# A planner's order searched anew with at most eight transfers in flight: attention and an MLP mixer on one core

## The chip, the cores and the metric

The kernel runs on one core of one Trainium2 chip. The metric is the device time of one execution in microseconds (us). Before the change three runs took 642.58, 644.96 and 646.78 us, so the median is 644.96 us.

## The reference, cut to what matters

Attention over 4 batches, 8 heads, 576 positions and head width 64, with a bias that a tiny network makes of the distance between positions; then a mixer over positions and an MLP over channels:

```python
scores = 0.125 * q @ k.T                          # per batch and head
x = log1p(abs(i - j)) / log1p(max(i, 1))          # 576 x 576
bias = relu(x[..., None] @ w1 + b1) @ w2          # 32 hidden, 8 heads; the same for all batches
attn = softmax(scores + bias)                     # sum + 1e-9 below the line
x = concat_heads(attn @ v)                        # 4 x 576 x 512, float32
h = relu(x.T @ w_tok1) @ w_tok2                   # mixes positions, 256 wide
u = x + h.T
out = u + relu(u @ w_ch1) @ w_ch2                 # 1536 wide; the weights are float64
```

## The kernel before, in words

All work goes through one planner. The program first lists steps (`add`), each with the engines that could run it and an estimated cost, a due time, the steps it comes after, and the buffers and PSUM banks that it takes and frees. `Plan.order` then plays the steps through on paper: at each turn it takes, on the engine that could start soonest, the step with the smallest due time among those that could start within `SLACK` of the first. The instructions are emitted in the order that comes out, so each engine's queue, SP's queue of transfers included, is fixed when the program is built. Nothing reorders at run time. Due times are the numbers of the table `DUE`, found by a search on the plan.

The stages, and the names that the text below uses:

- **Bias stage.** 36 blocks. For each, three rectifications on DVE (L494) and one on ACT (L492), 16 matmul instructions in the profile (L511), an eviction on ACT (L517) and a store of the block to DRAM (`bd<-slots`, L522). Meanwhile the k and q of the first units are loaded (L741, issued from ACT's queue) and split into a high part on ACT (L369: `kh`, `qh`) and a low part on DVE or POOL (L384: `kl`, `ql`).
- **Attention.** 16 units; a unit is one pair of heads of one batch. It loads k, q and v (`kk`, `qq`, `tv`, L741 and L745, from ACT's queue) and, for the first unit of a pair of heads, six pieces of the bias (`slots<-bd`, L716 and L719, from SP's queue). For each of five blocks of 128 rows: scores (L783), bias and row minimum on DVE (L792), exponential on ACT (L805), turning by transposing matmuls (L834, evicted by ACT at L837 and DVE at L840) or by a DMA transpose (L823), and the product with v (L861 to L863). Then the mixer over positions (L911 to L922), and the unit's result is stored (`um<-x`, L940, and `ul<-x`, L942, from SP's queue).
- **Weights.** Beside attention the float64 weights come in as words (L365, `keep<-wt`, `keep<-wc`) and are put together as float32 (L630, L632, L635, L638), their largest value taken (L359), and split.
- **Channels.** Five blocks of tokens. The stored rows are loaded, scaled and split (L1075, L1078), turned by DMA transposes (L1086), multiplied by the first weight (L1102 to L1104), and by the second (L1193 to L1195, or L1287 to L1289 with the reads at L1298 and L1301). Results leave at L1177.

Two things of the planner matter here. The first is how it treats a transfer: it assumes one wire on which transfers follow each other, and an issue costs its queue 0.4 us, or 0.35 us on ACT. The second is `keep_warm` (L318): where the plan has PE wait more than 1 us, it puts small matmuls of 128x256 on a free bank to fill that time.

In the built program every transfer, from either queue, signals one of eight semaphores in turn, and its issuing instruction first waits until the transfer that used that semaphore before has landed: about the one eight issues back, counted over both queues. This wait is in the program before and after the change; the planner before did not know of it.

Of the kernel before, what the change touches and what calls it, by code (L numbers as in the profile page):

```python
# [36 lines left out]
SLACK = 0.099  # L37
STAY = 136.61
# [17 lines left out]
      'dlo2': {'P': (1.9, 114.7), 'V': (0.67, -522.92)},  # L56
      'late': {'P': (0.7, 2520.57), 'A': (0.58, 2227.24)},
      'klow': {'P': (1.5, -153.69), 'V': (0.83, -54.59)},
      'zlow': {'P': (1.25, -1770.91), 'V': (0.6, 1857.34)},
      'twhole': {'P': (2.4, -3419.57), 'V': (1.21, -578.92)},  # L60
      'tsum': {'P': (3.0, 1762.24), 'V': (1.72, 444.73)},
      'tlow': {'P': (2.1, 1907.96), 'V': (1.15, 1327.33)},
      'oall': {'P': (2.7, 789.47), 'V': (1.2, 4220.75)},
      'norm': {'V': (0.35, -2033.47), 'A': (0.88, -1163.02)},
      'over': {'A': 0.65, 'V': (0.72, 409.34)},
      'vh': {'P': (0.7, 1664.84), 'V': (0.4, 1349.27), 'A': (0.6, 81.13)},
      'vl': {'P': (1.36, 488.82)}}
DUE = {'tie': 2658.62,
       'blk': -1001.52,
       'blkn': 37.41,  # L70
       'rect': -384.79,
       'bmm': -1271.54,
       'over': -2767.83,
       'put': -1632.04,
       'bl': 332.43,
       'bln': 47.87,
       'sums': 1060.11,
       'sumsn': 150.59,
       'measw': 219.61,
       'measwn': 13.46,  # L80
       'amax': 160.39,
       'scales': 261.94,
       'scalet': -1140.4,
       'scalec': -1768.42,
       'fill': -1334.98,
       'fill1': 1025.41,
       'tok': -998.98,
       'tokn': 86.58,
       'dec1': -291.1,
       'dec2': -123.37,  # L90
       'dec3': 843.13,
       'dec4': 377.41,
       'dec5': -1426.64,
       'load_k': 561.15,
       'load_q': -669.99,
       'split_k': -741.14,
       'first_k': -1091.54,
       'first_q': -317.21,
       'split_q': -105.53,
       'load_v': -1139.54,  # L100
       'prep_v': 2207.84,
       'prep_vh': -916.66,
       'prep_vl': -2285.41,
       'scores': -464.7,
       'biased': -310.8,
       'exp': -159.63,
       'hi': -1117.91,
       'lo': -515.95,
       'turn': -229.06,
       'flip': -1722.06,  # L110
       'fliphi': -1800.75,
       'flip2': -669.83,
       'fliplo': -46.83,
       'back': 1260.45,
       'norm': -696.83,
       'mix0': -1911.87,
       'mix1': 971.0,
       'relu': -3172.82,
       'mix2': -1913.89,
       'mix2b': -42.35,  # L120
       'store': -2510.07,
       'w1': 99.4,
       'w1n': 24.56,
       'U0': 902.85,
       'U0n': -448.96,
       'U1n': -76.52,
       'U1': 387.42,
       'U2': -1098.39,
       'Un': -26.37,
       'U3': 650.82,  # L130
       'U4': 532.91,
       'u1': 2642.21,
       'u2': -968.46,
       'u3': -735.61,
       'u4': -2938.78,
       'u5': 426.22,
       'G': 158.67,
       'G0': 1626.57,
       'G0n': -111.49,
       'g1': -1574.27,  # L140
       'g2': -177.12,
       'ur': -828.11,
       'H': 2543.86,
       'e1': 668.96,
       'e2': -24.44,
       'e3': -1194.05,
       'e4': 996.36,
       't2': 1217.88,
       't3': -1551.03,
       't4': -1836.99,  # L150
       'T1': -1314.84,
       'Tn': -167.36,
       'rd': 141.44,
       'urs': 643.45,
       'un': 116.14,
       'v1': -1357.25,
       'v2': 412.08,
       'v3': -88.48,
       'v4': -155.45,
       'v5': -1146.62,  # L160
       'v6': 564.59,
       'v7': -216.22,
       'v8': -2074.96,
       'w2m': -255.93,
       'w2mn': 54.04}
# [27 lines left out]
class Plan:  # L193
# [17 lines left out]
    def order(self):  # L211
        room = {k: [(0.0, i) for i in range(n)] for k, n in self.rooms.items()}
        at = dict(FIRST)
        wire, port, port_by = 4.0, 0.0, None
# [11 lines left out]
        while len(out) < len(self.steps):  # L226
            best = None
            for e, steps in ready.items():
                first, can = None, []
                for s in steps:  # L230
                    t = max(at[e], s.ready, *(h.busy[0] + (0.0 if h.busy[1] == e else 0.15) for h in s.bank))
                    if e == "P" or e == "V" and s.port:
                        t = max(t, port)
                    held = 0.0
# [33 lines left out]
            if s.wire:  # L268
                wire = max(wire, t + 0.56) + s.wire
                s.end = wire + (1.53 if s.gate else 1.93)  # L270
                at[e] = t + (ISSUE if e == "A" else 1.25 if s.gate else 0.4)
            else:
                if e == "P" and port_by is not None and port_by.engine == "V" and t <= port:
                    s.behind = port_by
                at[e] = s.end = t + cost
                if e == "P" or e == "V" and s.port:
                    port, port_by = s.end, s
# [18 lines left out]
def attention_mixer(ctx, tc, qT, kT, v, cst, lg, ident, wt1, wt2, wc1, wc2, out, dump=None):  # L296
# [111 lines left out]
    with tc.manual_schedule():  # L408
# [301 lines left out]
        def bias_load(hp, t0):  # L710
# [3 lines left out]
            for c in range(NCH):  # L714
                bias_in[hp, c] = [add(wire("bias", 2.0), t0 + DUE["bln"] * c,
# [14 lines left out]
        def unit(u):  # L730
# [37 lines left out]
            for c in range(NCH + 1):  # L768
# [17 lines left out]
                lead = chain("scores", add({"T": 0.9 if c < NCH else 0.95}, t + DUE["scores"], scores, after=[*ready, *bias_in[hp, c], drawn],  # L786
# [24 lines left out]
                if dma:  # L811
# [13 lines left out]
                    s = add({"A": 0.45}, t + DUE["hi"], rest_hi, after=exps[:1], take=[p2], use=[z])  # L825
# [571 lines left out]
```

## Time and profile before

| | us |
|---|---|
| median of 3 runs | 644.96 |
| lowest, highest | 642.58, 646.78 |
| profiled execution | 641.31 |
| its span on the core | 639.4 |
| PE busy | 617.8 (97%) |
| DVE busy | 501.8 (78%) |
| ACT busy | 410.0 (64%) |
| POOL busy | 266.4 (42%) |

The span reaches from the first instruction to the last; the remaining 1.9 us of the profiled execution lie around it. PE is TensorE's matmuls, DVE VectorE, ACT ScalarE, POOL GpSimd, SP the engine that only issues transfers; ACTq and SPq are the queues of ACT and SP. Idle time of an engine costs only where the end depends on it.

### The profile page before, as it was taken

How to read it: one execution, taken by the hardware profiler on the slowest of the kernel's cores; microseconds unless marked ns; L12 is line 12 of the kernel's file. 1: busy time of each engine (PE TensorE's matmuls, PEld its weight loads, DVE VectorE, ACT ScalarE, POOL GpSimd, SP SyncE). 2: the span in 40 equal slices, each digit the busy share in tenths (PEclk: the TensorE clock that was granted, in tenths of full speed). 3: DMA queues.
4: the chain of work that ended last, by engine and by line, in shares of the span. 5: the costliest groups of instructions: out<-in, count | busy, mean ns of one | idle time of the engine just before them, and what ended most of it. 6: DMA issues, size and time to landing. Idle time of an engine off the chain costs nothing.

```text
span 639.4 us, 18066 instructions
## 1 busy us (share of the span) xinstructions
PE 617.8 (97%) x7226; PEld 457.3 (72%) x7226; DVE 501.8 (78%) x1242; ACT 410.0 (64%) x751; POOL 266.4 (42%) x299
## 2 busy tenths in 40 slices
PE   9999888998999999999999999999999999999997
PEld 4445777896999998989899874444444468646886
DVE  7998899987899999999999867994775894266222
ACT  7998888876798999989888525542542641244110
POOL 1004777953575888778653700001233422022211
PEclk9999999998999999999999999999999999999999
DMA  8999665798676965466544795664221115400221
GB/s 314 403 365 336 132 143 146 264 332 191 192 160 194 287 125 138 112 144 185 132 95 86 240 290 213 180 176 116 52 64 40 63 34 132 99 1 0 81 86 33
DMA packets 88515, 101.92 MB, mean 159 GB/s; under 512 B 49392, under 2 KB 58864, under 8 KB 88432
## 3 DMA queue, kind: packets, MB, share of 16 engines
q1 hardware_dynamic: 78784, 80.04, 44.6%
q10 hardware_dynamic: 9648, 20.75, 11.1%
q8 instruction: 56, 0.92, 0.6%
q14 instruction: 27, 0.22, 0.1%
HBM read 69.69 MB, written 20.05 MB: 140 GB/s over the span
## 4 chain that ended last, share of the span: by engine, by line
PE 72%; DVE 9%; ACT 7%; DMA 5%; POOL 4%; issue 3%; ACTq 0%; SPq 0%; POOLq 0%; DVEq 0%
PE pair L783 7%; PE bank L834 6%; PE bank L1103 5%; PE bank L1104 5%; PE bank L1102 5%; PE bank L1289 4%; PE bank L1287 4%; PE bank L1288 4%; PE pair L511 4%; DVE z L792 3%; DVE t2a L840 2%; PE pair L1104 2%; PE bank L1195 2%; PE bank L1194 2%; PE pair L1103 2%
## 5 line engine op out<-in xcount | busy, mean ns | idle before, releaser
L805 ACT ACTIVATE z<-z,mx 128x576 f32<-128x576 f32 (+1 forms) x120 | 92.7, 780 | 12.1 <-DVE mx L792 7.6
L792 DVE CUSTOM_DVE_ANT_0 z<-pair,slots 128x576 f32<-128x576 f32 (+1 forms) x120 | 89.3, 756 | 4.2 <-PE pair L783 3.6
L840 DVE SCALAR_TENSOR_TENSOR t2a<-bank,t2a 128x384 f16<-128x384 f32 (+1 forms) x150 | 79.6, 538 | 6.6 <-ACT t2a L837 5.1
L834 PE MATMUL bank<-id,z 128*128 128x128 f32 x469 | 76.0, 283 | 6.2 <-DVE t2a L840 2.7
L837 ACT ACTIVATE t2a<-bank 128x384 f16<-128x384 f32 (+1 forms) x150 | 70.2, 473 | 16.8 <-PE bank L834 11.2
L783 PE MATMUL pair<-kh,qh 64*128 64x288 f32 (+1 forms) x288 | 62.5, 347 | 4.7 <-DVE mx L792 4.0
L834 PEld LDWEIGHTS bank<-id,z 128*128 128x128 f32 x469 | 50.0, 141 | 15.8 <-issue 4.8
L1103 PE MATMUL bank<-slots 128*128 128x512 f16 (+1 forms) x168 | 58.6, 349 | 1.3 <-DMA slots<-wd 1.3
L861 PE MATMUL bank<-vh,t2a 128*128 128x65 f16 x558 | 58.6, 194 | 0.0
L1102 PE MATMUL bank<-slots 128*128 128x512 f16 (+1 forms) x168 | 58.6, 349 | 0.0
L1104 PE MATMUL bank<-slots 128*128 128x512 f16 (+1 forms) x168 | 58.6, 349 | 0.0
L863 PE MATMUL bank<-vh,t2a 128*128 128x65 f16 x558 | 58.2, 192 | 0.1
L862 PE MATMUL bank<-vl,t2a 128*128 128x64 f16 x558 | 58.3, 191 | 0.0
L1298 DVE SCALAR_TENSOR_TENSOR slots<-bank,crow,slots 128x256 f32<-128x256 f32 x42 | 19.6, 481 | 43.2 <-PE bank L1289 34.2
L783 PE MATMUL pair<-kl,qh 64*128 64x288 f32 (+1 forms) x288 | 52.6, 299 | 0.0
L1232 POOL TENSOR_TENSOR me<-me 128x512 f32<-128x512 f16 x12 | 13.6, 1152 | 92.9 <-DVE wd L1078 76.2
L862 PEld LDWEIGHTS <-t2a 128*128 128x128 f16 x558 | 51.2, 98 | 0.6 <-issue 0.2
L861 PEld LDWEIGHTS <-t2a 128*128 128x128 f16 x558 | 51.1, 97 | 0.4 <-issue 0.2
L863 PEld LDWEIGHTS <-t2a 128*128 128x128 f16 x558 | 51.1, 97 | 0.2 <-DVE t2a L840 0.2
L783 PE MATMUL pair<-kh,ql 64*128 64x288 f32 (+1 forms) x288 | 50.9, 292 | 0.0
L783 PEld LDWEIGHTS pair<-kh,qh 64*128 64x128 f32 (+1 forms) x288 | 34.6, 185 | 16.8 <-DVE mx L792 7.6
L1104 PEld LDWEIGHTS <-slots 128*128 128x128 f16 x240 | 23.5, 98 | 24.7 <-issue 1.6
(271 smaller groups left out, 2037.2 us busy)
## 6 DMA issues: line engine op xcount, KB each, us to landing
keep<-wc SPq DMA_DIRECT2D x24, 512.0 KB, 4.2
wd<-wc SPq DMA_DIRECT2D x24, 512.0 KB, 4.7
bd<-slots SPq DMA_DIRECT2D x36, 288.0 KB, 6.4
slots<-bd SPq DMA_DIRECT2D x16, 576.0 KB, 6.9
slots<-v SPq DMA_DIRECT2D x8, 640.0 KB, 8.8
tv<-v ACTq DMA_DIRECT2D x16, 320.0 KB, 3.8
qq<-qT ACTq DMA_DIRECT2D x16, 320.0 KB, 4.2
kk<-kT ACTq DMA_DIRECT2D x16, 320.0 KB, 4.6
```

The costliest lines, as they stand in the source:

```text
L783: PE.matmul(out=pairs[both[h].i][:, 512 - i + n * i:512 + n * i], lhsT=qx[x][w, c * 128:c * 128 + 128], rhs=kx[y][w, k0:k0 + i], start=(j ...
L792: V.tensor_tensor_reduce(out=st["z"][z.i][:, o], in0=pairs[ph.i][:, 512 - i:512 + i], in1=bias_m[hp][:, c, h, :] if c < NCH else bias_l[hp ...
L805: A.activation(out=zz, in_=zz, func=ACTF.Exp, bias=mx_t[z.i][:, h:h + 1], scale=-1.0)
L834: PE.transpose(banks[tb.i][:, n * 128:(n + 1) * 128], st["z"][z.i][:, 384 * i + n * 128:384 * i + (n + 1) * 128], id32)
L837: A.activation(out=block(h.i, 0, m), in_=banks[tb.i][:, 0:128 * m], func=ACTF.Copy, scale=P_SCALE)
L840: V.scalar_tensor_tensor(out=block(h.i, 3, m), in0=banks[tb.i][:, 0:128 * m], scalar=P_SCALE, in1=block(h.i, 0, m), op0=ALU.mult, op1=ALU. ...
L861: PE.matmul(out=o, lhsT=lh, rhs=vh[:, n, 0:D + 1], start=(i == 0), stop=False)
L862: PE.matmul(out=ps[:, h, 0:D], lhsT=lh, rhs=vl[:, n, :], start=False, stop=False)
L863: PE.matmul(out=o, lhsT=ll, rhs=vh[:, n, 0:D + 1], start=False, stop=(i == 4))
L1102: PE.matmul(out=ps, lhsT=w[0][:, c], rhs=uh[:, c], start=(c == 0), stop=False)
L1103: PE.matmul(out=ps, lhsT=w[0][:, c], rhs=ul[:, c], start=False, stop=False)
L1104: PE.matmul(out=ps, lhsT=w[1][:, c], rhs=uh[:, c], start=False, stop=(c == 3))
```

## The change

The planner keeps the landing times of the last eight transfers (`lands`) and lets no transfer start before the one eight issues back has landed in its plan. Its estimate for a bias piece goes from 2.0 to 1.9 us. The dependence of work in the attention units on `drawn` (all 36 blocks' matmuls issued) is put where a shared buffer needs it: the first two scores of the first unit lose it, and the steps that write into turning buffers (L815, L834) get it. Every number of the tables `DUE` and `ON` that has to do with priority is new; the costs in `ON` are not. Two thresholds, `SLACK` and `STAY`, change too.

```diff
-SLACK = 0.099
-STAY = 136.61
+SLACK = 0.095
+STAY = 14.92
...
-       'load_k': 561.15,
+       'load_k': 593.08,
...
-       'first_k': -1091.54,
+       'first_k': -315.4,
...
-        wire, port, port_by = 4.0, 0.0, None
+        wire, port, port_by, lands = 4.0, 0.0, None, [0.0] * 4 + [4.0] * 4
...
                     if e == "P" or e == "V" and s.port:
                         t = max(t, port)
+                    if s.wire:
+                        t = max(t, lands[0])
...
             if s.wire:
                 wire = max(wire, t + 0.56) + s.wire
                 s.end = wire + (1.53 if s.gate else 1.93)
+                lands = lands[1:] + [s.end]
...
-                bias_in[hp, c] = [add(wire("bias", 2.0), t0 + DUE["bln"] * c,
+                bias_in[hp, c] = [add(wire("bias", 1.9), t0 + DUE["bln"] * c,
...
-                lead = chain("scores", add({"T": 0.9 if c < NCH else 0.95}, t + DUE["scores"], scores, after=[*ready, *bias_in[hp, c], drawn],
+                lead = chain("scores", add({"T": 0.9 if c < NCH else 0.95}, t + DUE["scores"], scores, after=[*ready, *bias_in[hp, c], *([drawn] if u or c > 1 else [])],
...
-                    s = add({"A": 0.45}, t + DUE["hi"], rest_hi, after=exps[:1], take=[p2], use=[z])
+                    s = add({"A": 0.45}, t + DUE["hi"], rest_hi, after=[exps[0], drawn], take=[p2], use=[z])
...
-                    s = chain("flip", add({"T": 0.11 * m + 0.02}, t + DUE["flip"] + DUE["flip2"] * i, flip, after=exps[:1 + (i > 0)], take=[tb, fb], free=[z]))
+                    s = chain("flip", add({"T": 0.11 * m + 0.02}, t + DUE["flip"] + DUE["flip2"] * i, flip, after=[*exps[:1 + (i > 0)], drawn], take=[tb, fb], free=[z]))
```

The rows of the two programs differ in order only: DVE, ACT, POOL and SP each have the same number of instructions of every line and shape. PE has 88 keep-warm matmuls where it had 82; the first 18 stand before the first block in both. The scores of the first unit still stand behind all blocks of the bias. Line numbers of the changed program are higher by three.

**SP's queue, the bias of the third pair of heads** (loaded while the second pair is at work; `bd_132` to `bd_136` are its pieces in DRAM, `um_126` to `um_129` the stores of the four batches, `wc` channel weights). Before:

```order
L716 DMA slots<-bd_132 128x1152
L716 DMA slots<-bd_133 128x1152
L716 DMA slots<-bd_134 128x1152
L716 DMA slots<-bd_135 128x1152
L719 DMA slots<-bd_136 64x576 x2
L940 DMA um_127<-x_84 128x4x128
L942 DMA ul_130<-x_84 64x128
L365 DMA keep<-wc 128x1024
L823 DMA_TRANSPOSE rect<-rect 128x6x128
L940 DMA um_128<-x_85 128x4x128
```

With the change:

```order
L943 DMA um_127<-x_84 128x4x128
L945 DMA ul_130<-x_84 64x128
L826 DMA_TRANSPOSE rect<-rect 128x6x128
L368 DMA keep<-wc 128x1024 x2
L826 DMA_TRANSPOSE rect<-rect 128x6x128
L719 DMA slots<-bd_132 128x1152
L943 DMA um_128<-x_85 128x4x128
L945 DMA ul_131<-x_85 64x128
L719 DMA slots<-bd_133 128x1152
L826 DMA_TRANSPOSE rect<-rect 128x6x128
L719 DMA slots<-bd_134 128x1152
L719 DMA slots<-bd_135 128x1152
```

The store of the second batch (`um_127`) stood behind all six pieces of the bias and now stands ahead of them; the pieces are spread between a store, weights and transposes.

**ACT's queue, the end of the bias stage** (the last evictions are L517 before, L520 with the change; `kh_103` and `qh_105` belong to the first unit, `kh_107` and `qh_109` to the second). Before, `kh_103` stands further up, among the evictions, and its `kk` was loaded well ahead of it. The end reads:

```order
L741 DMA kk<-kT 128x640
L517 ACTIVATE slots<-pair_64,slots 128x576
L492 ACTIVATE rect<-slots 128x576
L517 ACTIVATE slots<-pair_65,slots 128x576
L492 ACTIVATE rect<-slots 128x576
L517 ACTIVATE slots<-pair_64,slots 128x576
L369 ACTIVATE qh_109<-qq 128x640
L517 ACTIVATE slots<-pair_65,slots 128x576
L517 ACTIVATE slots<-pair_64,slots 128x576
L369 ACTIVATE kh_107<-kk 128x640
L517 ACTIVATE slots<-pair_65,slots 128x576
L344 ACTIVATE dggv<-id_73,mxgv 1x1
```

With the change:

```order
L495 ACTIVATE rect<-slots 128x576
L520 ACTIVATE slots<-pair_64,slots 128x576
L744 DMA kk<-kT 128x640
L520 ACTIVATE slots<-pair_65,slots 128x576
L520 ACTIVATE slots<-pair_64,slots 128x576
L520 ACTIVATE slots<-pair_65,slots 128x576
L372 ACTIVATE kh_103<-kk 128x640
L347 ACTIVATE dggv<-id_73,mxgv 1x1
```

The load of the first unit's k now stands three evictions ahead of its split, and the split behind the last eviction. The second unit's `kh_107` has moved behind the first exponentials. On DVE the first unit's `kl` follows the same way, behind L635, and the keep-warm matmuls between the last block and the first scores are 12 and 23, where there were none.

**DVE's queue, where the fifth block of tokens begins** (L1078 or L1081 is the low part of a split, L1298 or L1301 the read of a second product of the third and fourth blocks, L1142 or L1145 the first read of the fifth block's own products). Before:

```order
L1078 SCALAR_TENSOR_TENSOR wd<-me,mrut,keep 128x512
L1298 SCALAR_TENSOR_TENSOR slots<-bank_69,crow,slots 128x256
L1298 SCALAR_TENSOR_TENSOR slots<-bank_67,crow,slots 128x256
L1142 SCALAR_TENSOR_TENSOR me<-bank_66,me 128x512
```

With the change:

```order
L1081 SCALAR_TENSOR_TENSOR wd<-me,mrut,keep 128x512
L1301 SCALAR_TENSOR_TENSOR slots<-bank_69,crow,slots 128x256
L1301 SCALAR_TENSOR_TENSOR slots<-bank_67,crow,slots 128x256
L1301 SCALAR_TENSOR_TENSOR slots<-bank_68,crow,slots 128x256 x2
L1145 SCALAR_TENSOR_TENSOR me<-bank_69,me 128x512
```

One more product of an earlier block (18 matmuls on PE, read twice) stands between the last split of the fifth block and the fifth block's first products: on PE 324 matmuls of L1287 to L1289 stand ahead of those, where 306 did.

## Rows read from the trace of the kernel before

**Rows 1.** The page's busy times, and the keep-warm matmuls of L318.

```profile
PE 617.8 (97%) x7226; PEld 457.3 (72%) x7226; DVE 501.8 (78%) x1242; ACT 410.0 (64%) x751; POOL 266.4 (42%) x299
...
L318 PE MATMUL bank<-ones x82: 272/273/421, 1.0 to 156.1; 128*128 128x256 bf16 x82
```

**Rows 2.** Busy time by stretch: PE, PEld, DVE, ACT, POOL (instructions), PEclk, DMA share, GB/s.

```profile
40.00:60.00 20.00, 18.46 (x233) 9.09 (x226) 17.34 (x48) 18.05 (x29) 3.83 (x11) 1.00 0.96 334
60.00:120.00 60.00, 53.25 (x761) 45.20 (x760) 54.82 (x152) 52.14 (x100) 47.15 (x74) 1.00 0.60 155
120.00:140.00 20.00, 19.97 (x339) 18.41 (x336) 17.78 (x48) 14.89 (x28) 13.92 (x18) 1.00 1.06 342
140.00:150.00 10.00, 8.61 (x149) 7.76 (x145) 7.33 (x21) 6.09 (x13) 3.01 (x3) 1.00 1.13 298
150.00:160.00 10.00, 8.32 (x75) 6.82 (x76) 7.95 (x20) 8.28 (x16) 4.99 (x5) 0.83 0.55 162
160.00:350.00 190.00, 188.32 (x3238) 172.04 (x3236) 179.30 (x490) 169.10 (x320) 129.89 (x131) 1.00 0.64 155
350.00:550.00 200.00, 199.54 (x1348) 117.54 (x1345) 149.26 (x315) 86.04 (x160) 45.54 (x39) 1.00 0.46 130
550.00:560.00 10.00, 8.66 (x56) 5.21 (x55) 1.72 (x3) 1.15 (x3) 0.00 (x0) 1.00 0.47 118
```

**Rows 3.** Waits of 130 to 160 us: engine, line, releaser, total us, times, longest us.

```profile
ACT z L805 <- DMA um<-x: 3.9, 1, 3.9
...
PE bank L834 <- DVE rect L840: 2.5, 1, 2.5
```

**Rows 4.** Timeline of SP's queue and ACT: start us, us, engine, line, operation.

```profile
134.83 1.76 SPq L716 DMA_DIRECT2D slots<-bd  x4
...
138.25 0.48 SPq L940 DMA_DIRECT2D um<-x  x1
...
148.85 0.35 ACTq L741 DMA_DIRECT2D qq<-qT  x1
```

**Rows 5.** The chain that ended last, around the store: start us, us, what.

```profile
138.25 10.53 DMA um<-x
```

**Rows 6.** Tile kk in the first 60 us: its landing; the splits of k.

```profile
L369 ACT ACTIVATE kh<-kk x2: 728/738/747, 38.9 to 55.8; 128x640 fp32r<-128x640 f32 x2
L384 DVE TENSOR_TENSOR kl<-kk,kh x1: 826/826/826, 39.7 to 39.7; 128x640 fp32r<-128x640 f32 x1
...
DMA to landing us min/median/max: 6.6/6.7/6.8
```

**Rows 7.** Timeline of ACT, PE and DVE at the end of the bias stage.

```profile
51.76 0.73 ACT L517 ACTIVATE slots<-pair,slots 128x576 f32<-128x576 f32 x1
...
53.05 0.74 ACT L517 ACTIVATE slots<-pair,slots 128x576 f32<-128x576 f32 x1
...
56.40 0.73 ACT L517 ACTIVATE slots<-pair,slots 128x576 f32<-128x576 f32 x1
...
57.18 0.39 PE L783 MATMUL pair<-kh,qh 64*128 64x288 f32 x1 [0.39 <-ACT slots L517]
...
60.48 0.95 DVE L635 SCALAR_TENSOR_TENSOR keep<-keep 128x512 int32<-128x512 int32 x1
...
64.27 0.69 DVE L359 TENSOR_REDUCE m<-slots 128x1 f32<-128x512 f32 x1
```

**Rows 8.** The page's DMA issues: KB each, median us from issue to landing.

```profile
bd<-slots SPq DMA_DIRECT2D x36, 288.0 KB, 6.4
```

**Rows 9.** The chain that ended last, at the hole before the fifth block.

```profile
550.51 0.11 PE bank L1289
...
551.42 3.33 DMA slots<-wd
554.79 0.38 PE bank L1103
```

**Rows 10.** The page's groups: busy us, mean ns, idle us before and its releaser.

```profile
L1103 PE MATMUL bank<-slots 128*128 128x512 f16 (+1 forms) x168 | 58.6, 349 | 1.3 <-DMA slots<-wd 1.3
```

More of the change, by code (lines that the diff above doesn't have):

```diff
@@ L55 @@
 ON = {'dlo': {'P': 1.9},
[L56 to L93, printed above, removed]
-       'load_k': 561.15,
-       'load_q': -669.99,
-       'split_k': -741.14,
-       'first_k': -1091.54,
[L98 to L165, printed above, removed]
@@ new lines @@
+      'dlo2': {'P': (1.9, 414.99), 'V': (0.67, -150.29)},
+      'late': {'P': (0.7, 2701.14), 'A': (0.58, 2435.21)},
+      'klow': {'P': (1.5, -425.29), 'V': (0.83, -301.91)},
+      'zlow': {'P': (1.25, -1997.14), 'V': (0.6, 1630.86)},
+      'twhole': {'P': (2.4, -3355.5), 'V': (1.21, -585.86)},
+      'tsum': {'P': (3.0, 1707.32), 'V': (1.72, 156.46)},
+      'tlow': {'P': (2.1, 1128.03), 'V': (1.15, 422.71)},
+      'oall': {'P': (2.7, 894.77), 'V': (1.2, 4560.2)},
+      'norm': {'V': (0.35, -2043.09), 'A': (0.88, -927.36)},
@@ new lines @@
+      'over': {'A': 0.65, 'V': (0.72, 1477.48)},
+      'vh': {'P': (0.7, 1397.7), 'V': (0.4, 1248.08), 'A': (0.6, -369.06)},
+      'vl': {'P': (1.36, 766.2)}}
+DUE = {'tie': 2890.83,
+       'blk': -991.01,
+       'blkn': 44.48,
+       'rect': -394.37,
+       'bmm': -2158.07,
+       'over': -2846.53,
+       'put': -1646.85,
+       'bl': 565.64,
+       'bln': 64.77,
+       'sums': 325.9,
+       'sumsn': 190.71,
+       'measw': 164.73,
+       'measwn': 10.96,
+       'amax': 245.53,
+       'scales': -125.26,
+       'scalet': -1505.32,
+       'scalec': -499.0,
+       'fill': -2159.29,
+       'fill1': 787.6,
+       'tok': -1321.93,
+       'tokn': 27.31,
+       'dec1': -323.26,
+       'dec2': 363.56,
+       'dec3': 902.27,
+       'dec4': 402.88,
+       'dec5': -1671.28,
+       'load_k': 593.08,
+       'load_q': -668.85,
+       'split_k': -521.54,
+       'first_k': -315.4,
+       'first_q': -273.58,
+       'split_q': -171.64,
+       'load_v': -1302.39,
+       'prep_v': 2474.84,
+       'prep_vh': -937.02,
+       'prep_vl': -2139.16,
+       'scores': -131.78,
+       'biased': -447.3,
+       'exp': -281.64,
+       'hi': -431.18,
+       'lo': -499.34,
+       'turn': -183.71,
+       'flip': -1025.5,
+       'fliphi': -1239.59,
+       'flip2': -550.1,
+       'fliplo': -42.54,
+       'back': 133.24,
+       'norm': -440.16,
+       'mix0': -1365.07,
+       'mix1': 736.06,
+       'relu': -3896.1,
+       'mix2': -2223.46,
+       'mix2b': -35.73,
+       'store': -2800.38,
+       'w1': 42.77,
+       'w1n': 57.87,
+       'U0': 383.92,
+       'U0n': -340.06,
+       'U1n': -180.98,
+       'U1': 482.69,
+       'U2': -717.86,
+       'Un': 45.24,
+       'U3': -75.2,
+       'U4': 264.24,
+       'u1': 1778.4,
+       'u2': -233.72,
+       'u3': -692.99,
+       'u4': -2199.23,
+       'u5': -0.12,
+       'G': 353.73,
+       'G0': 1326.67,
+       'G0n': -61.15,
+       'g1': -880.12,
+       'g2': -70.08,
+       'ur': -528.11,
+       'H': 2976.09,
+       'e1': 476.58,
+       'e2': -218.17,
+       'e3': -859.37,
+       'e4': 1106.07,
+       't2': 871.03,
+       't3': -449.02,
+       't4': -1369.44,
+       'T1': -1687.29,
+       'Tn': -73.8,
+       'rd': -452.89,
+       'urs': 228.93,
+       'un': 143.47,
+       'v1': -1272.96,
+       'v2': 825.64,
+       'v3': -83.57,
+       'v4': 618.19,
+       'v5': -297.48,
+       'v6': 448.38,
+       'v7': 311.89,
+       'v8': -2607.96,
+       'w2m': -426.83,
+       'w2mn': 47.36}
```

## The prediction, on record before the changed kernel ran

> **What bounds the kernel now.** I read the busy times first, then the same by stretch, then the waits where PE has a hole, and then the chain through that hole. PE is busy 617.8 of 639.4 us [rows 1]; 82 of its matmuls, of about 0.27 us each and partly beside each other, are keep-warm filling, so "busy" contains some waiting. By stretch [rows 2] the kernel has three parts. From 160 to 350 us PE works 188.32 of 190 us and DVE 179.30: both are full. From 350 to 550 us PE works 199.54 of 200. What an order can win there is small. From 40 to 160 us PE is idle 1.54 + 6.75 + 0.03 + 1.39 + 1.68 = 11.4 us, and all keep-warm matmuls but those of the first 5 us lie ahead of 156 us [rows 1]. There DVE is the busiest of the others (54.82 of 60 us from 60 to 120). So the question is what the new order does to 40 to 160 us, and to the one hole later on, 1.34 us of idle PE at 550 to 560.
>
> The clearest hole begins at 145 us. ACT waits 3.9 us in one piece, and PE then 2.5 us [rows 3]. What ACT waits for is a ring, not data: it is about to issue the load of q, and the transfer eight or nine issues back, the second batch's store, has not landed. SP issued the bias pieces from 134.83 us and that store at 138.25 us, and ACT got its issue out at 148.85 us [rows 4]; the store took 10.53 us to land [rows 5], with the DMA engines at a share of 1.13 [rows 2]. This is what the planner did not know.
>
> **The change part by part.** No engine gets other instructions, so the sum consists of holes that close or open. It is made against the profiled execution, 641.31 us, which is 3.65 us below the median of the three runs, 644.96.
>
> *The ring wait at 145 us.* With the change the second batch's store stands ahead of the bias pieces, and these come one or two at a time between weights and transposes. The load of q that stood behind that store now has the third batch's small store eight back, with one bias piece issued shortly ahead of it instead of six. What the wait cost: PE idle 1.39 us in 140 to 150 and 1.68 us in 150 to 160, and a granted clock of 0.83 in the second stretch, which is 1.7 us of PE's time at full clock [rows 2]. That stretch ran partly at 1.2 GHz instead of 2.4, and what PE had done before was to stand idle for 2.5 us [rows 3]. Together 4.8 us; 160 to 350 us shows 0.1 us of idle in each 10 us where nothing is wrong, so 4.6 us are to be had. Bounds: 0, if the wait turns up elsewhere; 5.6 us, ACT's whole 3.9 us and the clock's 1.7. I take **-4.6**, because the order takes away exactly the queueing that the rows show.
>
> *The hole at 551 us.* PE waits there for the last transposes of the fifth block, 3.33 us on the chain [rows 9], of which 1.3 us is idle PE [rows 10]. The new order puts one more product of an earlier block ahead: 18 matmuls at 0.11 us (one piece of the chain in [rows 9]) make 2.0 us. The transposes and the transfers around them stand in the same order as before, so the hole is covered. Bounds 0 and 1.3; I take **-1.3**.
>
> *The start of attention.* Here the new order is worse. The first unit's k is loaded three evictions ahead of its split, where it had been loaded long before. Such a load took 6.6 to 6.8 us to land in this stage [rows 6]. Evictions come 1.29 us apart where a rectification stands between (51.76 and 53.05), and 0.73 us is one alone [rows 7], so three of them cover 2.2 to 3.9 us and ACT then waits 2.8 to 4.5 us. Behind it come the split on ACT, 0.74 us, and the low part on DVE, 0.83 us [rows 6], before the first scores can start. Before, these started at 57.18 us, right behind the last eviction at 56.40 [rows 7]. That is 4.4 to 6.1 us later, less two splits that no longer stand ahead of the last eviction (2 x 0.74): 2.9 to 4.6 us. In the gap DVE does work that it had to do later before: L635, 0.95 us, and L359, 0.69 us [rows 7], and DVE is what 60 to 120 us is made of [rows 2]; 1.6 us come back so. POOL too has weight work moved there. Bounds: 0, if everything that waits is filled; 4.6 us, if nothing comes back. I take **+2**: 1.3 to 3.0 with DVE's share returned. In the order the keep-warm matmuls say the same: 35 of them now stand between the last block and the first scores, about 3.9 us at the 0.11 us of a 256-column matmul [rows 9].
>
> The Trainium skill, "DMA: Bandwidth & Descriptors", section "Rules for kernel authors", advises to issue a DMA early and wait on its semaphore late. The change does the opposite with this load. The trace agrees so far as it goes: such a load lands 6.6 to 6.8 us after its issue [rows 6], so whoever reads it sooner waits.
>
> *The rest of 40 to 140 us.* 8.3 us of idle PE [rows 2] and some 60 keep-warm matmuls. They come from chains over DVE, ACT and POOL in an order that is now another, and nothing in the trace prices that. A bound below: half of that idle gone, -4. Above: one more wait of the size that PE had in the hole at 145 us, +2.5 [rows 3]. I take 0, as the new plan still puts 70 keep-warm matmuls behind the first block (64 before): the planner sees about as much waiting as it saw, though the ring is now in its sum.
>
> *From 160 us on*, apart from the hole: 0. PE is full [rows 2], its work is the same, and the last pieces stand in the same order. The six added keep-warm matmuls lie in the gap already counted.
>
> Sum: -4.6 - 1.3 + 2 + 0 = -3.9 us. On the profiled execution 637.4 us; on the median of three runs **641 us**. The least and the most of the terms together: -5.6 - 1.3 + 0 - 4 = -10.9, or 634; and 0 + 0 + 4.6 + 2.5 = +7.1, or 652.
>
> **The rivals.** About 1%, 6.4 us, is what a measurement of this kernel can tell from no change; so faster means below 638.5 and slower above 651.4.
>
> *More closes than the one hole* (634 us, chance 0.28). A plan that knows when transfers land orders everything around them better, and the gap at the start is filled completely: -10.9 as above. For it: DMA share is near 1 from 40 to 60 and from 120 to 150 us [rows 2], where the old plan was most wrong. Against it: of the waits from 130 to 160 us only one names a transfer [rows 3].
>
> *The wait only moves* (646 us, chance 0.15). The bytes are the same, the DMA engines are at a share above 1 from 120 to 150 us [rows 2], and ACT still issues loads of q, k and v whose turn in the ring falls on a store or a bias piece. If one of them blocks ACT for the same 3.9 us, only the hole at 551 goes: -1.3 + 2 = +0.7. Against it: fewer large transfers now stand together.
>
> *Slower: the first k* (651 us, chance 0.15). Its issue too has to wait for its turn: eight back is a store of a bias block, and these take 6.4 us to land [rows 8]. If it is held at ACT by 3 us, with the last three evictions behind it, the start costs 4.6 + 3 = 7.6 us; with the hole at 551 closed and the wait at 145 moved it comes to +6.3, or 651.3. It decides from the point where the start costs more than the 5.9 us that the two holes give back. Against it: before, this load was issued in the same stage and ACT went on at its pace. This is also what the Trainium skill's advice to issue early would have: with the k loaded early the start would cost nothing.
>
> **How the numbers follow.** Forecast 0.42, with a range of its own of 637 to 645; more closes 0.28; moves 0.15; slower 0.15. Faster by over 1%: 0.26 of the second case and 0.10 of the first, 0.36. Slower by over 1%: half of the last case and a little for what no row shows, 0.11. Within 1%: 0.53. The range from 632 to 650 leaves out the best end of the second case and the upper part of the last, together under 2 in 10.
>
> **What would show it.** ACT has no single wait of over 2 us on a transfer between 100 and 160 us, and the granted clock stays at 1.00 there. The hole at the fifth block is below 0.3 us. The first scores start 2.9 to 4.6 us after 57.18, with ACT waiting for `kk`. From 160 to 350 us PE's busy time is within 1 us of 188.3. I am wrong if the start costs over 6 us, if another load of q, k or v blocks ACT by the ring, or if PE opens holes after 160 us, above all where the second product begins, since no term of mine lies there.

## The result, and the profile after

The changed kernel took **636.54 us**, median of 4 runs (635.14 to 638.41), beside 643.88 us for the kernel before on the same chip (642.58 to 646.78): a ratio of 0.988 with an interval of 0.983 to 0.993. In two later sessions it took 635.34 us (5 runs, ratio 0.9864, 0.9845 to 0.9882) and 636.64 us (6 runs, 0.9882, 0.9853 to 0.9911). It is 1.2 to 1.4% faster. The forecast was 641 us, in a range from 632 to 650.

The profiled execution of the changed kernel took 638.41 us, the slowest of its four; that of the kernel before, 641.31 us, was faster than every timed run shown with it. So the two profiles are only 2.9 us apart, and a first task was to find where the other 4 us are.

Busy time by stretch after the change (columns as in [rows 2]):

```profile
40.00:60.00 20.00, 17.31 (x226) 8.21 (x219) 14.81 (x43) 16.89 (x27) 3.21 (x10) 1.00 0.95 317
60.00:120.00 60.00, 54.67 (x727) 45.60 (x725) 52.32 (x148) 49.08 (x93) 43.35 (x68) 0.94 0.59 158
140.00:150.00 10.00, 10.00 (x177) 9.21 (x174) 9.28 (x26) 9.04 (x18) 6.61 (x7) 1.00 1.13 325
150.00:160.00 10.00, 9.75 (x200) 8.65 (x197) 9.81 (x29) 8.24 (x17) 5.07 (x5) 1.00 1.10 339
160.00:350.00 190.00, 188.07 (x3216) 172.14 (x3217) 178.93 (x492) 169.05 (x319) 126.65 (x128) 1.00 0.64 152
550.00:560.00 10.00, 9.92 (x64) 5.98 (x62) 1.94 (x5) 2.59 (x5) 2.35 (x1) 1.00 0.39 101
```

Beside [rows 2]: from 140 to 160 us PE is busy for 19.75 us instead of 16.93, at a granted clock of 1.00 where the second half had 0.83, although the DMA share is higher in 150 to 160 (1.10, it was 0.55). The second batch's store, issued at 136.26 us, lands after 4.9 us where it took 10.53 [rows 5]. In the fifth block's stretch 0.08 us are idle. What got worse is 40 to 60 us, 1.15 us less busy, and the clock of 0.94 in 60 to 120: part of it ran at 1.2 instead of 2.4 GHz. Of ACT's waits (us in total, times, longest) the two largest in 100 to 160 us are no longer on a transfer, as those of [rows 3] were:

```profile
ACT z L808 <- DVE mx L795: 2.3, 4, 1.4
ACT z L808 <- POOL tv L754: 1.9, 1, 1.9
```

That store alone:

```profile
DMA to landing us min/median/max: 4.9/4.9/4.9
```

The start of attention, first on the chain that ended last (start, us, what), then on PE:

```profile
52.54 5.05 DMA kk<-kT
57.61 0.02 ACT kh L372
...
59.90 0.67 DVE keep L638
60.57 0.75 DVE kl L387
61.34 7.56 DMA kk<-kT
68.92 0.03 ACT kh L372
```

```profile
56.06 1.47 PE L321 MATMUL bank<-ones 128*128 128x256 bf16 x12
58.59 0.38 PE L348 MATMUL bank<-dggv,ones 1*128 1x1 f32 x2 [1.05 <-ACT dggv L347]
58.90 2.68 PE L321 MATMUL bank<-ones 128*128 128x256 bf16 x23
61.51 0.40 PE L786 MATMUL pair<-kh,qh 64*128 64x288 f32 x2
```

The first unit's `kk` is issued at 52.54 us and ACT splits it at 57.61; the low part waits on DVE behind a chain of weight work that ends with L638; the first scores start at 61.51 us, 4.3 us later than the 57.18 of [rows 7]. Then a thing that the prediction does not contain: there is one buffer `kk`, so the second unit's k can only be issued when the first's low part is done, at 61.34 us, and lands 7.56 us later. ACT's queue stands at that issue until 61.34 us; the wait of 4.0 us below is mostly this one, with 1.2 us more for POOL's L641, which had waited for the same low part. Then ACT stands before the second split, with exponentials and evictions behind it:

```profile
ACT keep L637 <- POOL slots L641: 4.0, 1, 4.0
ACT kh L372 <- DMA kk<-kT: 3.3, 2, 2.6
```

**Lost time.** To compare stretches I add up, for each matmul, the time from its start to the next one's start, less what its shape takes where nothing waits (the 30th percentile of the same shape in the run; for the bias blocks 66 ns and for the scores 82 ns); keep-warm matmuls count as lost altogether. It holds idle PE, the lower clock and filling in one number. Span less total is between 580.6 and 582.3 us in the five profiles below, so a total follows its span to 1.7 us only, and differences of 1 to 2 us between runs are weak evidence. The totals contain 0.2 to 0.3 us behind 570 us. In us, for two profiles of the kernel before and three of the changed one (the second of before and the last two of after are e5, e1 and e11 below):

```
stretch    before  e5     after  e1     e11
0-40        8.4    8.3     8.8    8.5    8.7
40-50       3.4    3.5     2.1    3.1    2.0
50-80      10.1   10.1    17.4   15.5   16.3
80-120     10.0   10.8     7.9    7.6    7.7
120-140     1.1    1.0     1.9    1.4    1.5
140-160     7.0    8.9     1.8    2.5    3.1
160-300     9.4    9.6     9.7   10.2   10.1
300-360     5.9    6.1     3.8    3.8    4.0
360-540     0.1    2.4     0.7    0.9    1.1
540-570     1.5    1.6     0.2    0.0    0.1
total      57.2   62.6    54.7   53.8   54.8
executed  641.31 646.72  638.41 637.01 637.19
```

### The profile page after: what moved, and what is told of

It is laid out like the page before. It is cut to its first block, busy times and chain, and to the rows that moved or that the text cites. A ratio compares the mean times of both kernels' runs of the same rounds, so it can differ in the third digit from the quotient of the medians.

```text
span 636.6 us, 18059 instructions
## 1 busy us (share of the span) xinstructions
PE 617.8 (97%) x7232; PEld 457.2 (72%) x7232; DVE 501.7 (79%) x1242; ACT 410.7 (65%) x751; POOL 267.1 (42%) x299
## 4 chain that ended last, share of the span: by engine, by line
PE 70%; DVE 12%; DMA 6%; ACT 5%; issue 2%; POOL 2%; SPq 1%; ACTq 0%; POOLq 0%; DVEq 0%
PE pair L786 7%; PE bank L837 7%; PE bank L1106 5%; PE bank L1107 5%; PE bank L1105 5%; PE bank L1291 4%; PE bank L1292 4%; PE bank L1290 4%; DVE z L795 3%; DMA kk<-kT 3%; DVE t2a L843 3%; PE pair L1106 2%; PE bank L1197 2%; PE bank L1196 2%; PE pair L1105 2%; PE pair L1107 2%
## 5 line engine op out<-in xcount | busy, mean ns | idle before, releaser
L837 PE MATMUL bank<-id,z 128*128 128x128 f32 x469 | 74.6, 283 | 4.5 <-ACT z L808 2.6
L1301 DVE SCALAR_TENSOR_TENSOR slots<-bank,crow,slots 128x256 f32<-128x256 f32 x42 | 19.6, 481 | 45.2 <-PE bank L1292 34.2
```

Of the source, the lines that this page charges most:

```text
L837: PE.transpose(banks[tb.i][:, n * 128:(n + 1) * 128], st["z"][z.i][:, 384 * i + n * 128:384 * i + (n + 1) * 128], id32)
```

## The experiments

**Theories.** A: the gain is the ring wait at 145 us and the hole at 551 us, the start of attention costs 7 us (by the first two profiles), and undoing it gives a kernel near 630 us. B: the start costs what was predicted, 2 us net, and the old kernel usually loses more than its first profile shows. C: the wait of 145 us only moves.

The order is cut and joined by number. In e2 to e4, e6, e7, e9 and e10 the planner is handed its 2,819 steps as a list of numbers and reckons times, buffers and filling as before; `before` and `after` below are the lists of the two kernels.

```diff
     def order(self):
-        room = {k: [(0.0, i) for i in range(n)] for k, n in self.rooms.items()}
...
+        return self.follow([int(x) for x in ORDER.split()])
```

**e1, the change again** (no edit).

> The changed kernel as it is, once more, so that what follows is compared on the same chip, and for a second profile of it: the profiled execution so far, 638.41 us, was the slowest of its four (the others 635.14 to 637.85). If the start of attention is what scatters (the loads of the first two k land at another time), the second profile shows its 3 us there, in 50 to 80 us; if the chip's state scatters, each stretch of 10 us is longer by a little. Median 636 to 637 us either way, 7 us below the kernel before.

Measured: 635.34 us (634.99 to 637.01; the profiled execution is the slowest, 637.01), a little below the 636 to 637 that was expected. The second profile is 1.4 us shorter than the first and loses 1.9 us less in 50 to 80 us; smaller differences elsewhere go both ways. The start does scatter.

**e2, the old start; e3, the new start; e4, the new order only around the ring wait.**

```diff
+e2: ORDER = before[:425], then what is left of after
+e3: ORDER = after[:425], then what is left of before
+e4: ORDER = before[:664], after up to 954 steps, then what is left of before
```

> The first 425 of the planner's 2819 steps (to about 80 us) stand in the order of the kernel before, the others in the new order. Theory: the start of attention in the new order costs about 7 us (50 to 80 us show 17.3 us of lost PE time after, 10.1 before, by the two profiles), since unit 0's k comes late and unit 1's k, which shares its buffer, later still. Then this kernel takes 629 to 631 us. Rival 1: the start costs the +2 us that was predicted, and the profile that was read is a slow example: 634 to 635 us. Rival 2: what follows depends on how the start went (DVE's weight work done in the gap comes back later): 636 to 638 us.

> The counterpart: the first 425 steps in the new order, the others as in the kernel before; the ring wait at 145 us and the hole at 551 us stay. Theory (the start costs 7 us): 650 to 651 us, slower than before by about 1%. Rival 1 (the start costs 2 us): 645 to 646 us. Rival 2 (the gap at the start is given back by work done in it): 643 to 644 us.

> Only the steps 664 to 954 (about 119 to 162 us) stand in the new order: the second batch's store ahead of the bias pieces and these spread. Start and end are those of the kernel before. Theory: the wait of ACT on the ring at 145 us, with PE's idle and half clock behind it, is gone and nothing takes its place: -4.6 to -5.3 us, 638.5 to 639.5 us, and no wait of ACT on a transfer of over 2 us in 120 to 160. Rival: the wait only moves to another load: 643 to 645 us, with such a wait in the profile.

Measured: e2 636.38 us (ratio 0.9884, 0.9867 to 0.9902), e3 650.18 (1.0102, 1.0079 to 1.0125), e4 642.25 (0.9975, 0.9959 to 0.9990). With the new start e3 is 5.7 us slower than the kernel before, yet the old start saves nothing in e2, and e4 gained 2 us where 4.6 to 5.3 were expected. The lost time says why. In e2 50 to 80 us lose 11.3 us, 4.2 less than in e1, but 80 to 120 us lose 10.3 instead of 7.6, as in the kernel before: what the new order does in the gap is still owed. Another 1.0 us goes in 20 to 30 us, where the planner set more filling (see e9). In e3 the start's 15.7 come with 12.2 in 160 to 300 and 2.3 in 380 to 400, which are no part of the start. In e4 the wait itself is gone (1.6 in 140 to 160), and 3.3 us more are lost in 160 to 300 than before, where POOL was idle ahead of a low part of q and the scores waited for it:

```profile
POOL ql L363 <- issue: 5.9, 1, 5.9
...
PE pair L762 <- POOL ql L363: 1.4, 1, 1.4
```

A piece of one plan set into another pays at its edges, so e3 and e4 don't price their parts. Theory A's 630 us did not come in e2; e7 and e9 below join the two orders where less is lost at the seam.

**e5, the kernel before again** (no edit, one execution).

> The kernel before as it is, for a second profile. Its profiled execution so far, 641.31 us, is below every one of its 17 timed runs (642.48 to 646.1, median 644.44), so the sum of the prediction was made against an execution 3 us too good. Theory: what varies is the wait on the ring, since it depends on when a store lands among six bias pieces; a profile of 643 to 646 us then shows its extra 2 to 4 us in 120 to 170 us, as longer waits of ACT on transfers. Rival: the 3 us lie elsewhere (the start, 160 to 350 us, the last wait for the output), or are spread over all stretches.

Measured: 646.72 us, 5.4 us above the first profile, and 5.4 us more lost time: 1.9 in 140 to 160, 2.3 in 360 to 540 and 0.8 in 80 to 120. So about a third lies where the theory had it and the rest elsewhere, as the rival had it. This execution is slower than all 20 timed ones beside it (640.91 to 645.70 us, median 644.15), of which three are below the first profile's 641.31: the two profiles stand near the two ends of the scatter.

```profile
ACT z L805 <- DMA um<-x: 5.0, 1, 5.0
...
PE bank L834 <- DVE rect L840: 3.5, 1, 3.5
```

```profile
150.00:160.00 10.00, 6.22 (x32) 4.76 (x34) 6.00 (x15) 7.46 (x14) 3.62 (x4) 0.70 0.83 187
...
380.00:400.00 20.00, 18.37 (x101) 9.47 (x99) 12.17 (x29) 7.47 (x15) 0.00 (x0) 1.00 0.79 274
```

The ring wait of [rows 3] took 5.0 us instead of 3.9, PE then stood for 3.5 instead of 2.5, and the clock that followed was 0.70. A second hole of 1.6 us at 390 us, where PE waits for DVE and DVE for the weights `wd<-wc`, was absent in the first profile. The changed kernel doesn't show the second hole in three profiles, and what is left of the ring wait there is 1.8 us at most (e11). The prediction had been worked out on an execution in which the first was the milder of the two and the second absent.

**e6, the six bias loads alone.** The kernel before, PE, DVE, ACT and POOL untouched; on SP:

```diff
-L716 DMA slots<-bd_132 128x1152
-L716 DMA slots<-bd_133 128x1152
-L716 DMA slots<-bd_134 128x1152
-L716 DMA slots<-bd_135 128x1152
-L719 DMA slots<-bd_136 64x576 x2
 L940 DMA um_127<-x_84 128x4x128
...
 L940 DMA um_128<-x_85 128x4x128
 L942 DMA ul_131<-x_85 64x128
+L716 DMA slots<-bd_133 128x1152
+L716 DMA slots<-bd_132 128x1152
 L823 DMA_TRANSPOSE rect<-rect 128x6x128
 L365 DMA keep<-wc 128x1024
+L716 DMA slots<-bd_134 128x1152
 L823 DMA_TRANSPOSE rect<-rect 128x6x128
+L719 DMA slots<-bd_136 64x576
+L716 DMA slots<-bd_135 128x1152
 L365 DMA keep<-wc 128x1024
 L823 DMA_TRANSPOSE rect<-rect 128x6x128
+L719 DMA slots<-bd_136 64x576
```

> The kernel before with one change: the six loads of the third head pair's bias pieces (SP, 134.83 us) stand later, behind the stores of the second and third batch and between transposes and weights, as in the new order; PE, DVE, ACT and POOL keep their order. Theory 1, by the profile of before: 140 to 160 us lose 7.0 us of PE time and 1.7 us would be normal, so 639 us. Theory 2, the wait on the ring is longer in the runs that are not profiled: 636 to 638 us. Rival: the wait moves to the bias pieces' readers or to the next loads: 643 to 645 us.

Measured: **638.89 us** (10 runs, 636.87 to 640.33; ratio 0.9932, 0.9910 to 0.9955), 5.3 us by the medians, 2.9 to 5.8 by the interval. From 140 to 160 us 3.9 us are lost, where the two profiles of before lose 7.0 and 8.9, and the clock is whole:

```profile
140.00:150.00 10.00, 10.00 (x200) 9.40 (x200) 8.97 (x26) 7.29 (x15) 3.01 (x3) 1.00 1.09 273
150.00:160.00 10.00, 9.03 (x107) 7.33 (x106) 8.49 (x22) 8.53 (x16) 5.18 (x6) 1.00 1.27 242
550.00:560.00 10.00, 8.74 (x46) 4.30 (x45) 2.14 (x5) 2.58 (x5) 0.00 (x0) 1.00 0.26 66
```

The ring wait is shorter, not gone. The load of q is issued at 148.31 us, 0.08 us after a transpose landed that had used its semaphore before, and ACT stands for 1.7 us around it (3.9 and 5.0 before). The profile names DVE for that wait:

```profile
148.31 0.33 ACTq L741 DMA_DIRECT2D qq<-qT  x1
148.69 0.83 ACT L805 ACTIVATE z<-z,mx 128x640 f32<-128x640 f32 x1 [1.71 <-DVE x L895]
```

The time is what theory 1 said, though 3.9 us are still lost where it had 1.7. Of the 5.3 us, 3.2 to 5.0 stand in this place, by the two profiles of before; where the rest lies is not shown. Theory C is refuted as to the time: most of the wait went, and none of its size took its place. The hole at 551 us stays, as it must here (1.26 us idle).

**e12, the same six loads put back in front, in the changed kernel.**

```diff
-        for s in plan.order():
+        six, o = plan.steps[1221:1227], plan.order()
+        o = [s for s in o if s not in six]
+        for k, s in enumerate(six):
+            o.insert(754 + 4 * k, s)
+        for s in o:
```

> The changed kernel with the six bias loads put back in front of the second batch's store, all else unchanged. The turn in the ring comes out another way than in the kernel before: the transfer whose landing ACT's load of q now waits for is a load of weights issued eight back, not that store. Theory 1, the bytes in front are what counts (each transfer behind six pieces lands late, whoever waits for it): 140 to 160 us lose 5 us more, 640 to 642 us. Theory 2, the wait came from ACT's load falling on the store's turn: 635 to 637 us, no wait of ACT on a transfer over 2 us.

Measured: 643.77 us (12 runs, 639.54 to 648.93; ratio 0.9993), 7.1 us above the changed kernel beside it. 140 to 160 us lose 9.5 us. ACT's load is no longer the one that is stopped. SP itself is, twice in a row, on the chain:

```profile
126.18 8.15 DMA kk<-kT
...
134.35 0.32 SPq L719
...
134.71 7.28 DMA slots<-bd
...
142.00 0.03 SPq L826
...
142.07 10.56 DMA rect<-rect
```

A bias piece waits until a `kk` in the ring has landed, a transpose until that piece has, and PE waits 5.3 us for the transposed block:

```profile
PE bank L864 <- DMA rect<-rect: 6.5, 2, 5.3
...
140.00:150.00 10.00, 4.70 (x74) 4.38 (x72) 2.98 (x10) 3.14 (x6) 1.99 (x2) 0.70 1.04 175
```

Theory 1 holds against theory 2: with the six pieces in front, that store took 11.8 us to land and the time of the kernel before is back, though another engine is stopped. The cost is even above the 640 to 642 us that were expected. What e11 adds below is that a late landing doesn't need the six pieces.

**e10, the six loads later and the new order from 480 us on.**

```diff
+e10: ORDER = (list of e6)[:2504], then what is left of after
```

> The kernel before with the six bias loads later, as in the run that moved only these, and from step 2504 on (about 480 us) the new order, in which a product of the earlier block stands ahead of the fifth block's first ones. The hole at 551 us, 1.4 to 1.6 us in every profile of the old order, should be gone: 638.9 less 1.4, 637.5 us. Rival: the wait for the weights moves to the next product and the time stays 638.9 us; the stretch 550 to 560 us tells.

Measured: **636.64 us** (6 runs, 635.45 to 638.67; ratio 0.9894, 0.9866 to 0.9922). PE is busy in the whole of 550 to 560 us (10.00) and 540 to 570 us lose 0.2. This kernel, with the old start and the old order up to 480 us but for six loads, takes what the changed kernel beside it takes, 636.64 us. It came 0.9 us lower than expected: the step from e6, 2.3 us, is more than the hole's 1.3, but the two intervals overlap. Its profile, the slowest of its six (638.67 us), loses 3.3 us in 360 to 540, as e5's lost 2.4: that hole comes and goes in the old order.

**e7 and e9, the old start joined where the two plans nearly agree.**

```diff
+e7: ORDER = before[:630], then what is left of after
+e9: as e7, and in follow():
-            if s.wire:
+            if s.wire and len(out) >= 630:
                 t = max(t, lands[0])
```

> The first 630 steps (to about 113 us) in the order of the kernel before, the others in the new order: the old start without the seam at 80 us of the run before, where ACT waited 1.9 us for POOL's weight work and 80 to 90 us lost 4.4 us instead of 1.9. If the late k's cost is real and only the seam hid it, 50 to 80 us lose 10 us instead of 15.5 and 80 to 113 us what they lose in the kernel before (7 instead of 6): 631 to 632 us. If the weight work that the new start does in the gap is owed later, what the start saves returns by 120 us: 635 to 636 us, the changed kernel's time.

> As the run with the old order to about 113 us, but the keep-warm matmuls of that stretch are those of the kernel before (the planner's ring rule, by which it places them, counts only from step 630 on). With the rule it had put eight of them ahead of a block at about 25 us, and 20 to 30 us lost 1.3 us instead of 0.3. If they were in the way, 1 us comes back: 634 us, the fastest so far. If PE would have waited there anyway: 635 us.

Measured: e7 635.15 us (ratio 0.9888, 0.9861 to 0.9916), e9 634.71 us (634.30 to 636.25; 0.9863, 0.9837 to 0.9889). The start of e7 beside that of the change, 60 to 80 and 80 to 120 us, first e7, then the changed kernel:

```profile
60.00:80.00 20.00, 18.42 (x225) 15.45 (x224) 17.11 (x46) 16.56 (x30) 15.64 (x36) 1.00 0.74 184
80.00:120.00 40.00, 36.80 (x520) 31.90 (x517) 36.82 (x109) 33.52 (x65) 29.99 (x36) 0.87 0.53 153
```

```profile
60.00:80.00 20.00, 16.36 (x115) 12.83 (x114) 14.19 (x33) 11.64 (x22) 12.10 (x33) 0.83 0.59 179
80.00:120.00 40.00, 38.30 (x614) 32.77 (x613) 38.12 (x116) 37.43 (x73) 31.25 (x36) 1.00 0.59 147
```

What the late k costs before 80 us comes back behind it: 50 to 80 us lose 10.1 us in e7 and 15.5 in e1, 80 to 120 us 11.1 and 7.6. Net of 40 to 120 us: 24.6 against 26.2, and 23.8 in e9 against 26.0 in e11. So the new start is dearer by 1.6 to 2.2 us in lost time; counted from 0 us, where e7 and e9 lose 0.9 us more than e1 and e11, it is 0.8 and 1.3 us, within what the measure can tell. The times don't separate it: e9 stands 1.9 us below the change beside it, with overlapping intervals, and e7 is level with e1 of the earlier session. Theory A's 630 us is refuted: 634.71 us is the nearest. Theory B's 2 us fit, but are not shown by a time. In e9 the filling taken from 20 to 30 us (1.3 to 0.3 lost) turned up as waiting in 30 to 40 (0.8 to 2.1): its rival was right. e9 is the fastest median of the study, not shown to be faster than the change.

**e8, the rule alone.**

```diff
+                    if s.wire:
+                        t = max(t, lands[0])
...
+                lands = lands[1:] + [s.end]
```

> The kernel before with the rule alone: the planner holds each transfer until the one eight issues back has landed; the numbers of the tables, and what the first products and flips wait for, are those of before. The whole order comes out anew. If the rule is what gains, the bias pieces of the third head pair no longer stand in front of a store that ACT's load waits for, and 140 to 160 us lose 2 us instead of 7: 637 to 640 us. If the numbers found under the old rule don't fit the new one, holes open elsewhere: 643 to 650 us.

Measured: 647.71 us (11 runs; ratio 1.0065, 1.0042 to 1.0088), slower than before.

```profile
60.00:120.00 60.00, 53.48 (x696) 44.34 (x695) 50.00 (x141) 46.63 (x88) 42.22 (x66) 0.94 0.61 169
...
140.00:150.00 10.00, 9.77 (x193) 8.94 (x190) 8.72 (x25) 8.56 (x18) 7.45 (x8) 1.00 1.10 300
...
160.00:350.00 190.00, 184.96 (x3131) 167.50 (x3129) 177.65 (x480) 166.76 (x317) 127.08 (x128) 1.00 0.59 150
```

Both expectations were half right. The rule does close the ring wait (1.4 us lost in 140 to 160) and half of the hole at 551 (0.7 left in 540 to 570), and it brings the late start (16.9 in 50 to 80). But with numbers found without it 120 to 140 lose 3.9 and 160 to 300 us 13.3: PE works 184.96 us of 190 where it had 188.32. The rule alone is not enough. The rest of the change (the new numbers, the moved dependence on `drawn`, the 1.9 us for a bias piece) was not taken apart, and new numbers without the rule were not run; by hand, e10 gets the same time without either.

**Last profile of the change (e11),** beside e9, e10 and e12:

> The changed kernel once more, on the same chip as the runs beside it, and for a third profile: 635 to 636 us. Its profiles so far show 1.2 and 2.1 us lost in 150 to 160 us and 15.5 to 17.3 us in 50 to 80; a third tells how far these vary.

Measured: 636.64 us, a little above the 635 to 636 expected; its lost time stands in the table above. 140 to 160 us vary between 1.8 and 3.1, 50 to 80 between 15.5 and 17.4. The variation in 140 to 160 goes with the third batch's store, which has one bias piece shortly before it: it lands after 7.5 us in the first profile, 11.4 in e1 and 12.2 in e11. The load of q whose turn falls on the small store behind it then stops ACT for 1.3 us in e1 and here for 1.8:

```profile
153.57 0.33 ACTq L744 DMA_DIRECT2D qq<-qT  x1
154.01 0.49 ACT L840 ACTIVATE t2a<-bank 128x384 f16<-128x384 f32 x1 [1.85 <-DMA ul<-x]
```

So a store can land as late without six pieces in front of it, at a DMA share of 1.1 in 140 to 160 us in all three profiles. What the new order changes is whose turn falls on a late landing, and for how long.

## Why the prediction was right or wrong

The direction was right, and so were the causes of the two terms that gain. The time came out 4.4 to 5.7 us lower than the forecast, inside its range but below the forecast's own 637 to 645 and outside its likeliest class (faster by over 1% had 0.36).

*The sum itself* came out. It said 637.4 us for a profiled execution, starting from 641.31; the three of the change took 638.41, 637.01 and 637.19. That it agrees so well is partly luck. By lost time, from that first profile to the mean of the three, the ring wait gave 4.5 us and the hole 1.4, as forecast, but 40 to 120 us cost 3.0 instead of 2; 300 to 360 us gave 2.0 that no term had, and the other stretches cost 2.2 that no term had: -2.7 us in all, of the 3.8 us by which the executions differ. The step that failed is the next one, "on the median of three runs 641 us": the 3.65 us between the profile of before and its median were carried over as a constant, and the medians moved by 7.3 us, not by 3.9. Of the miss of 4.5 us, 1.1 lay in the start: a fourth run put the median of before at 643.88 instead of 644.96. For the rest, e5 shows where a slow execution of the kernel before loses more than the profile that I used: 1.9 us more at the ring, 2.3 in 360 to 540 us and 0.8 in 80 to 120. The first of these the change shortens and the second it doesn't show; how much of them a median execution has is not shown. The change's own profiles lie 0.5 to 1.9 us above their medians.

*The ring wait, -4.6.* Right in cause: moving the six loads alone gave -5.3 us by medians (e6), putting them back +7.1 (e12). Its size is known less well than these two numbers look: in the place itself, 140 to 160 us, e6 loses 3.2 to 5.0 us less than the kernel before, the change 5.5 less on average (7.0 and 8.9 before, 1.8 to 3.1 after). The bound of 5.6 was taken from the one wait of 3.9 us and is too low for an execution like e5's. And the mechanism is wider than I put it. In e12 it is SP's transposes that are held, and PE waits for these. And the wait is not gone with the change: the load of q has its turn on the third batch's small store, as I said, and stood 1.3 and 1.8 us for it in e1 and e11. I treated the store's 10.53 us as the work of the pieces in front of it; e1 and e11 show 11.4 and 12.2 us with one such piece shortly in front.

*The hole at 551 us, -1.3.* Right: 1.5 and 1.6 us lost before, with PE's wait for the last transposes as in [rows 10], 0.0 to 0.2 after; e10, which takes it over with the end of the order, loses 0.2.

*The start, +2.* Its net size fits lost time (0.8 to 2.2 us by e7 and e9, 2.5 by the means of the table), which is too coarse to show it, and the first scores came 4.3 us later, within the 2.9 to 4.6. The way there was another, so that agreement is luck in part. The first k landed after 5.05 us, not 6.6, so ACT waited 0.72 us for it instead of 2.8 to 4.5; what held the scores was the low part, which stood on DVE behind weight work until 60.57 us. I left out the one buffer `kk`: the second load had to follow that low part, so ACT's queue stood at its issue, and it took 7.56 us. That makes 6.3 us of lost time in 50 to 80 us (means of the table), above my bound of 4.6. My test, "wrong if the start costs over 6 us", calls this wrong as a gross cost; but 2.7 us return in 80 to 120 and 1.1 in 40 to 50, by the way that was named, work of DVE and POOL done in the gap. The Trainium skill, "DMA: Bandwidth & Descriptors", section "Rules for kernel authors", advises to issue a load early and wait for it late. The trace agrees for the place itself, 5.05 and 7.56 us from issue to landing with ACT waiting at the end of both; the time of the kernel hardly followed, as other work was there to fill.

*The rest of 40 to 140 us, 0*: apart from what belongs to the start, 0.5 us more are lost in 120 to 140.

*From 160 us on, 0*: wrong by 2 us in a place that I called full. 300 to 360 us lose 6.0 us before and 3.9 after. The hole at 312 us, where a scores matmul waited for DVE (0.66 us idle), is gone, and that at 353 us is smaller. It goes with the new order in that stretch: e7 and e9, which have it, lose 3.8 and 3.9 us, e6 and e10, which have the old, 5.6 and 5.8. Which of the changed numbers does it no run here isolates. PE's busy time in 160 to 350 us, my test, stayed within 0.3 us and hid it.

*The rivals.* "The wait only moves" is refuted by e6 as to the time; what it named does happen, at 1.3 to 1.8 us instead of 3.9. "The first k held by the ring" did not occur: `kk` was issued between two evictions without a wait. "More closes" came nearest in time (634), for another reason than its own: the gap at the start was not filled.

**Open:** the medians differ by 7.3 to 9.1 us and the profiles, on the average of two and three, by 644.0 - 637.5 = 6.5. What the fastest executions of the change (634.2 to 635.5) do differently no profile shows.

## What to carry to other kernels

Where a few semaphores are shared in turn by all transfers, a block of large loads that nobody needs soon can delay what comes behind it, on either queue, and the wait is shown at a load or a transpose that has nothing to do with it, or is put down to another engine. Look up which transfer had the semaphore before, and move the block alone before touching anything else. If the timed runs scatter by 1%, take a second profile before predicting, and see where each stands among the timed runs: a wait that varies was 1.1 us longer in the second here. Numbers found under one rule of a planner can lose under another (e8): a rule without a new search is not a test of the rule.

## What was unexpected on the chip

The same program's wait on the same landing took 3.9 us in one execution and 5.0 in another, and the granted clock in the ten us that followed was 0.83 and 0.70: with a wait 1.1 us longer, 140 to 160 us lost 1.9 us more. The same store of the third batch took 7.5, 11.4 and 12.2 us to land in three executions of one program. In e12 a transpose issued at 142.07 us behind six bias pieces took 10.56 us to land.
